# Strassen's seven half products for b in two of six pairs of ft tiles

## The chip, the cores and the metric

The kernel runs on one core of a Trainium2 chip. The metric is the device time of one execution in microseconds (us). Five engines work beside each other, each with its own in-order queue: TensorE (PE; PEld are its weight loads), VectorE (DVE), ScalarE (ACT), GpSimd (POOL), and SyncE (SP), which here issues nearly all DMAs.

## The reference

Chunked attention without a mask between chunks, then a bilinear feed-forward layer. Heads are merged to the 512 model columns, and all products are plain matrix products:

```python
# q, k, v: (8, 8, 576, 64), chunks of 64 rows
scores = scale * np.matmul(q_c, k_c.transpose(0, 1, 2, 4, 3))
scores = scores - np.max(scores, axis=-1, keepdims=True)
attn = np.exp(scores)
attn = attn / (np.sum(attn, axis=-1, keepdims=True) + 1e-09)
out = np.matmul(attn, v_c)
...
# x: (4608, 512) from out; w_a, w_b: (512, 1536); w_out: (1536, 512)
a = x @ w_a
b = x @ w_b
return (a * b @ w_out).astype(np.float32)
```

## The kernel before

The 4608 tokens are cut into nine blocks of 512 (K = 0 to 8), and each block into two units of 256 tokens (u = 0 to 17). Attention of a unit gives half of xT, the block's x with model columns on the partitions (four tiles of 128, index kt). Of the 1536 hidden columns there are twelve ft tiles of 128, held in six pairs of 256 (wa, wb, wo, ab2).

Each block takes fourteen steps, s = 0 to 13. In steps 0 to 11 `ffn(K, ft)` makes one ft tile: four matmuls of 512 columns for b into one PSUM bank, four for a into the next (`ffn_products`, L399), then `ffn_close`: ScalarE casts b's bank to the bf16 tile bsb (L410), and VectorE multiplies a's bank by it into ab (L411). After every odd step VectorE makes `sum_ab` of the pair that is complete (L466 to L468), three sums that the output needs. In steps 12 and 13 `outs_fast` makes the output by Strassen's seven products of half size, with sums of ab and wo, 42 matmuls of 256 columns a step (L479), two copies by ScalarE, five adds by VectorE and three by GpSimd (L497). So the output product already has the form that the change gives to part of b.

All these products take their PSUM banks from a ring of four, F, in the order in which `nextF()` is called:

```python
    F = [pp.tile([128, 512], FP32, name=f"F{i}") for i in range(4)]
```

A product may start only when the bank that was handed out four requests earlier has been read. Semaphores for this and for all data are set from the order in which the program names the instructions; nothing is reordered, so the order within each engine's queue is the order of the program.

Attention of the next block lies between the steps. From block 3 on, `slot` comes after steps 1 and 8 (in block 2 after 4 and 9). It takes two banks of F for the sums of the exponentials (L252), makes the values into a separate bank pair PA (L268), has ScalarE take two logarithms (L278) and one reciprocal by the exponential (L282), and makes the scores of the following unit (L235). What comes behind it is put into a list `late`, and `step()` at the head of each following step issues one piece: the first normalise by VectorE (L287), the second, then ScalarE's exponential (L246):

```python
                    inverse(uv)
                    late.extend([(normalise, (uv, 0)), (normalise, (uv, 1))])
            if us is not None:
                scores(us, pairs)
                late.append((expo, (us,)))
```

A step after a slot GpSimd casts the q, k and v of the unit after next from f32 to bf16 (`cast_unit`, L170, 128x1024 each); two steps later SP issues the transposing DMA of q and k (`turn_unit`) and the loads of a later unit (`load_unit`).

Blocks 0 and 1 run an older form of the loops, with the loading of the weights, and are not touched by the change. The staging buffer wsta of the weights, ten parts of 1024 f32 columns, is taken over after that by wsum and asum, the sums for the outputs, in its parts 2 to 9; parts 0 and 1 lie idle.

Of the kernel before, what the change touches and what calls it, by code (L numbers as in the profile page):

```python
# [11 lines left out]
def kernel(  # L12
# [10 lines left out]
    nc = tc.nc  # L23
    BF16 = mybir.dt.bfloat16
    FP32 = mybir.dt.float32
    AF = mybir.ActivationFunctionType
    MULT = mybir.AluOpType.mult
    ADD = mybir.AluOpType.add
    SUB = mybir.AluOpType.subtract
# [7 lines left out]
    NKT = DM // 128  # L37
    NFT = DFF // 128
    BLK = 512
    NBLK = NTOK // BLK  # L40
    NU = NTOK // 256
# [5 lines left out]
    def buf(name, shape, dt):  # L47
        return sb.tile(shape, dt, name=name)
# [4 lines left out]
    for K in range(NBLK):  # L53
        if K == REST:
            chunks += [(b, 512) for b in range(B)]
        else:
            b = K if K < REST else K - 1
# [19 lines left out]
    xT = [buf(f"xT_{i}", [128, NKT, BLK], BF16) for i in range(3)]  # L77
# [5 lines left out]
    ab = [ab2[i // 2][:, i % 2, :] for i in range(NFT)]  # L83
    wa = [buf(f"wa_{i}", [128, NKT, 256], BF16) for i in range(NP)]
    wb = [buf(f"wb_{i}", [128, NKT, 256], BF16) for i in range(NP)]
    wo = [buf(f"wo_{i}", [128, 2, DM], BF16) for i in range(NP)]
    NWS = 10
    wsta = buf("wst", [128, NWS * 1024], FP32)
# [8 lines left out]
    asum = wsta[:, 6 * 1024:10 * 1024].bitcast(BF16)[:, 0:NP * 5 * HF]  # L97
    asum = asum.rearrange("p (i n t) -> p i n t", i=NP, n=5)
    part = buf("part", [128, 2, 5, HF], FP32)

    state = {"f": 0, "b": 0, "o": 0, "w": 6}

    def ring(name, bufs):
        i = state[name]
        state[name] = i + 1
        return bufs[i % len(bufs)]

    def nextF():
        return ring("f", F)
# [63 lines left out]
    def cast_qk(u, x, eng):  # L173
        copy(eng, qkb[u % 2][:, x, :], f32[u % NF32][x])
# [11 lines left out]
    def cast_v(u, eng, pieces=1):  # L186
        n = 1024 // pieces
        for i in range(pieces):
            copy(eng, vb[u % 3][:, n * i:n * i + n], f32[u % NF32][2][:, n * i:n * i + n])
# [203 lines left out]
    def ffn_products(K, ft, us, kts, banks, of="ba"):  # L393
        n = 256 * len(us)
        x = xT[K % 3]
        for m in of:
            w, bank = (wb, banks[0]) if m == "b" else (wa, banks[1])
            for kt in kts:
                nc.tensor.matmul(  # L399
                    bank[:, 0:n],  # L400
                    w[ft // 2][:, kt, (ft % 2) * 128:(ft % 2) * 128 + 128],
                    x[:, kt, us[0] * 256:us[0] * 256 + n],
                    start=(kt == 0),
                    stop=(kt == NKT - 1),
                )
# [9 lines left out]
    def ffn(K, ft, us=(0, 1)):  # L415
        banks = nextF(), nextF()
        ffn_products(K, ft, us, range(NKT), banks)
        ffn_close(K, ft, us, banks)
# [40 lines left out]
            c0, c1, op = ((1, 3, SUB), (2, 0, SUB), (0, 3, ADD))[part - 1]  # L459
            eng.tensor_tensor(out=y[:, part + 1], in0=b[:, c0], in1=b[:, c1], op=op)  # L460

    def sum_ab(i):

        a = ab2[i].rearrange("p f (h t) -> p (f h) t", h=2)
        y = asum[:, i]
        nc.vector.tensor_tensor(out=y[:, 4], in0=a[:, 0], in1=a[:, 3], op=ADD)  # L466
        nc.vector.tensor_tensor(out=y[:, 0:2], in0=a[:, 0:2], in1=a[:, 2:4], op=ADD)  # L467
        nc.vector.tensor_tensor(out=y[:, 2:4], in0=a[:, 1:3], in1=a[:, 0:4:3], op=SUB)  # L468

    def outs_fast(K, t):  # L470
        c = t * 128
        m3, m4, w, y1, y2 = [part[:, t, n, :] for n in range(5)]
        oa, ob = ring("o", osb), ring("o", osb)
        V, A, G = nc.vector, nc.scalar, nc.gpsimd

        def product(a, b, o=None, pairs=range(NP)):
            o = nextF()[:, 0:HF] if o is None else o
            for i in pairs:
                nc.tensor.matmul(  # L479
                    o, a(i)[:, c:c + 128], b(i), start=(i == 0), stop=(i == NP - 1)  # L480
                )
            return o

        def of_ab(f, h):
            return lambda i: ab2[i][:, f, h * HF:(h + 1) * HF]

        def of_wo(f, h):
            return lambda i: wo[i][:, f, h * HF:(h + 1) * HF]

        def of_asum(n):  # L490
            return lambda i: asum[:, i, n]

        def of_wsum(n):
            return lambda i: wsum[:, i, n]

        def add(eng, out, in0, in1, op=ADD):
            eng.tensor_tensor(out=out, in0=in0, in1=in1, op=op)  # L497

        if K == NBLK - 1 and t == 1:

            A.copy(out=m3, in_=product(of_ab(0, 0), of_wsum(2)))
            A.copy(out=m4, in_=product(of_ab(1, 1), of_wsum(3)))
            add(G, w, m3, m4)
            add(V, oa[:, HF:DM], product(of_asum(0), of_wo(1, 1)), m3)
            add(G, y1, w, oa[:, HF:DM], SUB)
            add(V, ob[:, 0:HF], product(of_asum(1), of_wo(0, 0)), m4)
            add(G, y2, w, ob[:, 0:HF], SUB)
            p1 = product(of_asum(4), of_wsum(4))
            store(K, 2 + t, ob, 0, HF)
            add(V, y1, p1, y1)  # L510
            add(V, oa[:, 0:HF], product(of_asum(3), of_wsum(1)), y1)
            store(K, t, oa)
            add(V, y2, p1, y2)
            add(V, ob[:, HF:DM], product(of_asum(2), of_wsum(0)), y2)
            store(K, 2 + t, ob, HF)
            return
        A.copy(out=m3, in_=product(of_ab(0, 0), of_wsum(2)))

        p4 = product(of_ab(1, 1), of_wsum(3), None, range(NP - 1))
        p1 = product(of_asum(4), of_wsum(4), None, range(NP - 1))  # L520
        product(of_ab(1, 1), of_wsum(3), p4, (NP - 1,))
        product(of_asum(4), of_wsum(4), p1, (NP - 1,))
        A.copy(out=m4, in_=p4)  # L523
        add(G, w, m3, m4)
        add(V, w, p1, w)
        add(V, oa[:, HF:DM], product(of_asum(0), of_wo(1, 1)), m3)
        add(G, y1, w, oa[:, HF:DM], SUB)
        add(V, ob[:, 0:HF], product(of_asum(1), of_wo(0, 0)), m4)
        add(G, y2, w, ob[:, 0:HF], SUB)
        add(V, oa[:, 0:HF], product(of_asum(3), of_wsum(1)), y1)  # L530
        store(K, t, oa)
        add(V, ob[:, HF:DM], product(of_asum(2), of_wsum(0)), y2)
        store(K, 2 + t, ob)
# [16 lines left out]
    with tc.manual_schedule():  # L550
# [4 lines left out]
        V, A, G = nc.vector, nc.scalar, nc.gpsimd  # L555
# [123 lines left out]
        def load_unit(u, xs=(0, 1, 2)):  # L679
            for x in once("load", u, xs):  # L680
                load_natural(u, x, (q, k, v)[x], nc.sync)

        def cast_unit(u, xs=(0, 1, 2)):
            for x in once("cast", u, xs):
                if x < 2:
                    cast_qk(u, x, G)
                else:
                    cast_v(u, G)

        def turn_unit(u):  # L690
            for _ in once("turn", u, (0,)):
                transpose_dma(u, nc.sync)
# [11 lines left out]
        def slot(uv, us, pairs=False, short=False):  # L704


            drain()
            if uv is not None:
                SU = nextF(), nextF()
                sums(uv, SU)  # L710
                values(uv)
                log_sums(uv, SU)
                if short:
                    for cl in range(2):
                        late.extend([(inverse, (uv, cl)), (normalise, (uv, cl))])
                else:
# [6 lines that stand above are left out]
        def step():  # L723
            if late:
                fn, a = late.pop(0)
                fn(*a)
# [45 lines left out]
        for f0 in range(0, NFT, 2):  # L772

            for tgs in ((0, 1), (2, 3)):
# [3 lines left out]
                if (f0, tgs[0]) == (2, 0):  # L778
                    t = [transpose_pairs(2, x, (PS, PA)[x][:, 0, :]) for x in range(2)]
# [83 lines left out]
        slots = {}  # L863
        for K in range(2, NBLK):
            for s0, u in zip((4, 9) if K == 2 else (1, 8), (2 * K + 3, 2 * K + 4)):
                slots[K * (NFT + 2) + s0] = u
        for K in range(2, NBLK):
            for s in range(NFT + 2):
                step()
                if s < NFT:  # L870
                    ffn(K, s)
                    if s % 2:
                        sum_ab(s // 2)
                else:
                    outs_fast(K, s - NFT)
                if (K, s) == (2, 0):
                    slot(None, 6)
                i = K * (NFT + 2) + s
                if i in slots and slots[i] - 1 < NU:
                    slot(slots[i] - 1, slots[i] if slots[i] < NU else None)  # L880
                if i - 1 in slots:

                    cast_unit(slots[i - 1] + 1, (0, 1) if slots[i - 1] == 8 else (0, 1, 2))
                if i - 5 in slots:
                    cast_unit(slots[i - 5] + 1)
                if i - 3 in slots:
                    turn_unit(slots[i - 3] + 1)
                    load_unit(slots[i - 3] + 3)


# [28 lines left out]
```

## Time and profile before

| | |
|---|---|
| median of three runs | 314.49 us (312.73 to 314.68) |
| the profiled execution | 314.75 us, its span 313.0 us |
| TensorE busy | 303.3 us, 97% |
| VectorE busy | 187.1 us, 60% |
| ScalarE busy | 135.0 us, 43% |
| GpSimd busy | 124.4 us, 40% |
| granted TensorE clock | 1.000 |

In the lines of the profile, a row of a group names the line, engine and operation, what is written and read, the shapes, the count, the busy time, the mean of one in ns, and after the second bar the idle time of the engine before these instructions with its releaser. A row of the timeline gives the start in us from the span's start, the duration, the engine and line, and in brackets the time that the engine stood idle before. A row of the chain gives start, duration, engine and line. Matmul records overlap, since matmuls are pipelined; a pace is read from the distance of starts.

### The profile page before, as it was taken

The numbers are of one execution on the slowest core, as the hardware profiler recorded it, in microseconds if no ns is written. First come the engines' busy times: TensorE is split into PE (matmuls) and PEld (weight loads), VectorE is DVE, ScalarE is ACT, GpSimd is POOL, SyncE is SP. The second block draws the span as 40 slices with busy tenths as digits, with TensorE's granted clock in tenths as the row PEclk, the third lists the DMA queues.
The fourth block names the chain that finished last, engine by engine and source line by source line (L and its number), as shares of the span: only waits on it lengthen the run. The fifth ranks groups of instructions, "written<-read, shape, count | busy, mean of one in ns | idle before, by whom it ended". The sixth has DMA issues, their size and how long they took to land.

```text
span 313.0 us, 7353 instructions
## 1 busy us (share of the span) xinstructions
PE 303.3 (97%) x2924; PEld 177.9 (57%) x2924; DVE 187.1 (60%) x373; ACT 135.0 (43%) x232; POOL 124.4 (40%) x155
## 2 busy tenths in 40 slices
PE   7898989999999999999999999999999999999995
PEld 3433446885444486447644764467446744674474
DVE  3543324544449664966496749674967476646664
ACT  3833236746236533553265326541644164413320
POOL 2676857966666137402630264016500400040013
PEclk9999999999999999999999999999999999999999
DMA  7999999999999999989699239933500320021003
GB/s 260 282 310 385 376 281 259 224 219 266 233 225 265 225 222 259 238 191 199 208 246 237 55 137 212 240 88 136 134 2 2 82 55 0 3 90 46 0 1 136
DMA packets 144915, 55.01 MB, mean 176 GB/s; under 512 B 126320, under 2 KB 138864, under 8 KB 144880
## 3 DMA queue, kind: packets, MB, share of 16 engines
q1 hardware_dynamic: 143792, 53.49, 68.3%
q10 hardware_dynamic: 1088, 1.05, 1.0%
q8 instruction: 23, 0.38, 0.5%
q14 instruction: 12, 0.10, 0.1%
HBM read 37.75 MB, written 9.44 MB: 151 GB/s over the span
## 4 chain that ended last, share of the span: by engine, by line
PE 85%; DMA 9%; SPq 3%; DVE 1%; issue 1%; POOL 0%; ACTq 0%; DVEq 0%
PE F L399 53%; PE F L479 20%; PE F L421 6%; DMA f<-in_k_dram 5%; DMA wst<-in_moe_w_b_dram 4%; SPq L155 2%; PE F L252 2%; PE PS L235 2%; PE PA L268 1%; SPq L147 1%; SPq L160 0%; POOL wb L170 0%; ACTq L140 0%; PE F L195 0%; DVE osb L497 0%
## 5 line engine op out<-in xcount | busy, mean ns | idle before, releaser
L399 PE MATMUL F<-xT,wa 128*128 128x512 bf16 (+1 forms) x472 | 115.0, 361 | 1.3 <-POOL wa L170 1.0
L399 PE MATMUL F<-xT,wb 128*128 128x512 bf16 (+1 forms) x472 | 115.4, 361 | 0.9 <-DVE xT L385 0.9
L410 ACT CAST bsb<-F 128x512 bf16<-128x512 f32 (+1 forms) x118 | 64.4, 547 | 104.6 <-PE F L399 104.4
L411 DVE TENSOR_TENSOR ab<-F,bsb 128x512 bf16<-128x512 f32 (+1 forms) x118 | 75.7, 643 | 52.1 <-PE F L399 38.0
L399 PEld LDWEIGHTS <-wa 128*128 128x128 bf16 x472 | 45.9, 98 | 50.2 <-POOL wa L170 3.2
L399 PEld LDWEIGHTS <-wb 128*128 128x128 bf16 x472 | 44.6, 98 | 43.7 <-POOL wb L170 0.8
L497 POOL TENSOR_TENSOR part<-part 128x256 f32<-128x256 f32 x14 | 10.1, 724 | 129.7 <-ACT part L523 128.6
L170 POOL CAST qkb<-f 128x1024 bf16<-128x1024 f32 (+1 forms) x35 | 34.6, 1002 | 24.1 <-DMA f<-in_q_dram 13.8
L479 PEld LDWEIGHTS <-wst 128*128 128x128 bf16 x420 | 41.1, 98 | 4.8
L287 DVE TENSOR_TENSOR xT<-PA,inv 128x512 bf16<-128x512 f32 x32 | 21.8, 684 | 19.4 <-ACT inv L282 19.4
L479 PE MATMUL F<-wst 128*128 128x256 bf16 x252 | 33.3, 273 | 0.0
L497 DVE TENSOR_TENSOR osb<-F,part 128x256 f32<-128x256 f32 x56 | 22.4, 420 | 11.2 <-POOL part L497 9.7
L497 POOL TENSOR_TENSOR part<-part,osb 128x256 f32<-128x256 f32 x28 | 19.7, 725 | 11.4 <-DVE osb L497 11.3
L170 POOL CAST vb<-f 128x1024 bf16<-128x1024 f32 (+2 forms) x22 | 20.1, 917 | 10.0 <-DMA f<-in_v_dram 10.0
L479 PE MATMUL F<-wst,ab 128*128 128x256 bf16 x168 | 22.8, 273 | 0.0
L467 DVE TENSOR_TENSOR wst<-ab 128x512 bf16<-128x512 bf16 x42 | 22.3, 530 | 0.0
L421 PE MATMUL F<-wo,ab 128*128 128x512 bf16 x96 | 21.7, 379 | 0.0
L468 DVE TENSOR_TENSOR wst<-ab 128x512 bf16<-128x512 bf16 x42 | 21.4, 510 | 0.0
L246 ACT ACTIVATE E<-PS 128x1024 bf16<-128x1024 f32 (+1 forms) x20 | 18.8, 942 | 5.1 <-PE PS L235 3.5
L278 ACT ACTIVATE lns<-F 128x512 f32<-128x512 f32 x30 | 16.3, 595 | 10.3 <-PE F L252 10.3
L479 PE MATMUL F<-wo,wst 128*128 128x256 bf16 x168 | 20.6, 273 | 0.0
L497 DVE TENSOR_TENSOR part<-F,part 128x256 f32<-128x256 f32 x15 | 6.4, 424 | 21.1 <-POOL part L497 21.1
(62 smaller groups left out, 195.5 us busy)
## 6 DMA issues: line engine op xcount, KB each, us to landing
out_dram<-osb SPq DMA_DIRECT2D x31, 256.0 KB, 2.6
f<-in_q_dram SPq DMA_DIRECT2D x28, 256.0 KB, 4.1
f<-in_v_dram SPq DMA_DIRECT2D x28, 256.0 KB, 4.7
f<-in_k_dram SPq DMA_DIRECT2D x24, 256.0 KB, 4.2
wst<-in_moe_w_out_dram SPq DMA_DIRECT2D x6, 512.0 KB, 8.8
f<-in_v_dram SPq DMA_DIRECT2D x16, 128.0 KB, 3.8
wst<-in_moe_w_b_dram SPq DMA_DIRECT2D x8, 256.0 KB, 5.2
wst<-in_moe_w_a_dram SPq DMA_DIRECT2D x8, 256.0 KB, 5.2
```

Source lines behind the costliest of these rows:

```text
L170: eng.tensor_copy(out=out, in_=in_)
L246: nc.scalar.activation(out=e[:, :, s], in_=PS[:, :, s], func=AF.Exp, scale=scale)
L278: nc.scalar.activation(out=lns[:, cl, :], in_=SU[cl], func=AF.Ln)
L287: nc.vector.tensor_tensor(out=x.rearrange("p m (g c t) -> p c g m t", g=2, c=2)[:, cl], in0=PA[:, cl, :].rearrange(shape, g=2, m=4), in1=i ...
L399: nc.tensor.matmul(bank[:, 0:n], w[ft // 2][:, kt, (ft % 2) * 128:(ft % 2) * 128 + 128], x[:, kt, us[0] * 256:us[0] * 256 + n], start=(kt ...
L410: nc.scalar.copy(out=bT[:, 0:n], in_=banks[0][:, 0:n])
L411: nc.vector.tensor_tensor(out=ab[ft][:, us[0] * 256:us[0] * 256 + n], in0=banks[1][:, 0:n], in1=bT[:, 0:n], op=MULT)
L421: nc.tensor.matmul(o, ab[ft][:, tg * 128:(tg + 1) * 128], wo[ft // 2][:, ft % 2, :], start=(ft == 0), stop=(ft == NFT - 1),)
L467: nc.vector.tensor_tensor(out=y[:, 0:2], in0=a[:, 0:2], in1=a[:, 2:4], op=ADD)
L468: nc.vector.tensor_tensor(out=y[:, 2:4], in0=a[:, 1:3], in1=a[:, 0:4:3], op=SUB)
L479: nc.tensor.matmul(o, a(i)[:, c:c + 128], b(i), start=(i == 0), stop=(i == NP - 1))
L497: eng.tensor_tensor(out=out, in0=in0, in1=in1, op=op)
```

## The change

In blocks 3 to 8, b of the pairs 1 and 3 (ft tiles 2, 3 and 6, 7) is no longer made by four matmuls a tile. x is cut into halves of its tokens and of its model columns, the pair's weights into halves of model columns and of the two tiles, and b of both tiles is made by Strassen's seven products of half size, two matmuls of 256 columns each. `fast_b` does it in four stages, each with one bank of F:

- stage 0: two products; ScalarE copies both to f32, GpSimd adds them into m1
- stage 1: two products; VectorE adds them to the copies, into the middle half of bS
- stage 2: one product; VectorE adds it to m1, GpSimd makes two differences y12
- stage 3: two products; VectorE adds them to y12, into the outer quarters of bS

`with_b` then makes a of each of the two tiles as before, and VectorE multiplies it by bS, which is f32 and lies in SBUF; for these tiles there is no cast of b's bank. The stages lie between the other tiles in a list `work` of fourteen steps. The sums of weights are made once a pair by `sum_w` on GpSimd (pair 1 in block 2 at step 9, pair 3 at its end), the sums of x once a block by `sum_x`, also on GpSimd: 1 and 2 at step 11 of the block before, 0 and 3 at step 0. `sum_ab` can be issued in parts, and the list `ab_sums` says where. From block 3 on the casts of q and v go to ScalarE, q one step and v four steps after the cast of k, which stays on GpSimd. Block 2 keeps its order apart from the added sums.

```diff
+    spare = wsta[:, 0:2 * 1024].bitcast(BF16)
+    SP = (1, 3)
+    ws = {p: spare[:, i * 1280:i * 1280 + 1280].rearrange("p (n k c) -> p n k c", n=5, k=2)
+          for i, p in enumerate(SP)}
+    xs3 = spare[:, 2560:4096].rearrange("p (n k t) -> p n k t", n=3, k=2)
+    xs2 = buf("xs2", [128, 2, 2, 256], BF16)
+    xs = [xs3[:, 0], xs3[:, 1], xs3[:, 2], xs2[:, 0], xs2[:, 1]]
+    bS = buf("bS", [128, 2 * BLK], FP32)
...
-    def sum_ab(i):
+    def sum_ab(i, parts=(4, 0, 2)):
...
-        nc.vector.tensor_tensor(out=y[:, 4], in0=a[:, 0], in1=a[:, 3], op=ADD)
-        nc.vector.tensor_tensor(out=y[:, 0:2], in0=a[:, 0:2], in1=a[:, 2:4], op=ADD)
-        nc.vector.tensor_tensor(out=y[:, 2:4], in0=a[:, 1:3], in1=a[:, 0:4:3], op=SUB)
+        V = nc.vector
+        for part in parts:
+            if part == 4:
+                V.tensor_tensor(out=y[:, 4], in0=a[:, 0], in1=a[:, 3], op=ADD)
+            elif part == 0:
+                V.tensor_tensor(out=y[:, 0:2], in0=a[:, 0:2], in1=a[:, 2:4], op=ADD)
+            else:
+                V.tensor_tensor(out=y[:, 2:4], in0=a[:, 1:3], in1=a[:, 0:4:3], op=SUB)
+    def sum_w(p, eng):
+        w, y = wb[p], ws[p]
+        for out, in0, in1, op in (
+            (y[:, 0:2].rearrange("p n k c -> p k n c"),
+             w[:, 0:2].rearrange("p k (n c) -> p k n c", n=2),
+             w[:, 2:4].rearrange("p k (n c) -> p k n c", n=2), ADD),
+            (y[:, 2], w[:, 0:2, 0:128], w[:, 2:4, 128:256], ADD),
+            (y[:, 3], w[:, 0:2, 128:256], w[:, 0:2, 0:128], SUB),
+            (y[:, 4], w[:, 2:4, 0:128], w[:, 2:4, 128:256], SUB),
+        ):
+            eng.tensor_tensor(out=out, in0=in0, in1=in1, op=op)
+    def sum_x(K, n, eng):
+        x = xT[K % 3]
+        a, b = x[:, :, 0:256], x[:, :, 256:512]
+        out, in0, in1, op = (
+            (xs[0], a[:, 0:2], b[:, 2:4], ADD),
+            (xs[1], b[:, 0:2], b[:, 2:4], SUB),
+            (xs[2], a[:, 2:4], a[:, 0:2], SUB),
+            (xs2.rearrange("p n k t -> p (n k) t"), a, b, ADD),
+        )[n]
+        eng.tensor_tensor(out=out, in0=in0, in1=in1, op=op)
+    def fast_b(K, p, stage):
+        x, w, y = xT[K % 3], wb[p], ws[p]
+        V, A, G = nc.vector, nc.scalar, nc.gpsimd
+        m = part[:, SP.index(p)]
+        m34, m1, y12 = m[:, 0:2], m[:, 2], m[:, 3:5]
+        b4 = bS.rearrange("p (n c) -> p n c", n=4)
+        bank = nextF()
+        def product(h, a, b):
+            for k in range(2):
+                nc.tensor.matmul(
+                    bank[:, h * 256:h * 256 + 256], a[:, k], b[:, k], start=(k == 0), stop=(k == 1)
+                )
+        both = bank.rearrange("p (n c) -> p n c", n=2)
+        if stage == 0:
+            product(0, w[:, 0:2, 0:128], xs[1])
+            product(1, w[:, 2:4, 128:256], xs[2])
+            A.copy(out=m34, in_=both)
+            G.tensor_tensor(out=m1, in0=m34[:, 0], in1=m34[:, 1], op=ADD)
+        elif stage == 1:
+            product(0, y[:, 0], x[:, 2:4, 256:512])
+            product(1, y[:, 1], x[:, 0:2, 0:256])
+            V.tensor_tensor(out=b4[:, 1:3], in0=both, in1=m34, op=ADD)
+        elif stage == 2:
+            product(0, y[:, 2], xs[0])
+            V.tensor_tensor(out=m1, in0=bank[:, 0:256], in1=m1, op=ADD)
+            for n in range(2):
+                G.tensor_tensor(out=y12[:, n], in0=m1, in1=b4[:, 1 + n], op=SUB)
+        else:
+            product(0, y[:, 4], xs[4])
+            product(1, y[:, 3], xs[3])
+            V.tensor_tensor(out=b4[:, 0:4:3], in0=both, in1=y12, op=ADD)
+    def with_b(K, ft):
+        bank = nextF()
+        ffn_products(K, ft, (0, 1), range(NKT), (None, bank), "a")
+        c = (ft % 2) * BLK
+        nc.vector.tensor_tensor(out=ab[ft], in0=bank, in1=bS[:, c:c + BLK], op=MULT)
...
+        def queue_next_fast(i):
+            if i - 1 in slots:
+                cast_unit(slots[i - 1] + 1, (1,))
+            if i - 2 in slots:
+                cast_unit(slots[i - 2] + 1, (0,), A)
+            if i - 5 in slots:
+                cast_unit(slots[i - 5] + 1, (2,), A)
+            if i - 3 in slots:
+                turn_unit(slots[i - 3] + 1)
+                load_unit(slots[i - 3] + 3)
...
+            if s == 9:
+                sum_w(SP[0], G)
+            if s == NFT - 1:
+                sum_x(3, 1, G)
+                sum_x(3, 2, G)
...
+        sum_w(SP[1], G)
+        p, r = SP
+        work = [
+            [(ffn, 0), (fast_b, p, 0)],
+            [(ffn, 1)],
+            [(fast_b, p, 1), (fast_b, p, 2), (ffn, 4)],
+            [(fast_b, p, 3), (with_b, 2)],
+            [(with_b, 3), (fast_b, r, 0)],
+            [(ffn, 5)],
+            [(fast_b, r, 1), (fast_b, r, 2), (ffn, 8)],
+            [(fast_b, r, 3), (with_b, 6)],
+            [(with_b, 7)],
+            [(ffn, 9)],
+            [(ffn, 10)],
+            [(ffn, 11)],
+            [(outs_fast, 0)],
+            [(outs_fast, 1)],
+        ]
+        ab_sums = {4: [(0,)], 5: [(1,)], 6: [(2,)], 8: [(3, (4, 0))], 10: [(4, (4, 0))],
+                   11: [(5, (4, 0)), (3, (2,)), (4, (2,)), (5, (2,))]}
+        for K in range(3, NBLK):
+            for s, todo in enumerate(work):
+                step()
+                if s == 0:
+                    sum_x(K, 0, G)
+                for fn, *args in todo:
+                    fn(K, *args)
+                if s == 0:
+                    sum_x(K, 3, G)
+                if s == NFT - 1 and K + 1 < NBLK:
+                    sum_x(K + 1, 1, G)
+                    sum_x(K + 1, 2, G)
+                for a in ab_sums.get(s, ()):
+                    sum_ab(*a)
                 i = K * (NFT + 2) + s
+                slot_at(i)
+                queue_next_fast(i)
```

More of the change, by code (lines that the diff above doesn't have):

```diff
@@ L681, in load_unit, with cast_unit @@
                 load_natural(u, x, (q, k, v)[x], nc.sync)
-        def cast_unit(u, xs=(0, 1, 2)):
+        def cast_unit(u, xs=(0, 1, 2), eng=G):
             for x in once("cast", u, xs):
                 if x < 2:
-                    cast_qk(u, x, G)
+                    cast_qk(u, x, eng)
                 else:
-                    cast_v(u, G)
+                    cast_v(u, eng)
         def turn_unit(u):
@@ L866, with queue_next @@
                 slots[K * (NFT + 2) + s0] = u
-        for K in range(2, NBLK):
-            for s in range(NFT + 2):
-                step()
[L870 to L877, printed above, removed]
-                i = K * (NFT + 2) + s
[L879 to L888, printed above, removed]
+        def queue_next(i):
+            if i - 1 in slots:
+                cast_unit(slots[i - 1] + 1, (0, 1) if slots[i - 1] == 8 else (0, 1, 2))
+            if i - 5 in slots:
+                cast_unit(slots[i - 5] + 1)
+            if i - 3 in slots:
+                turn_unit(slots[i - 3] + 1)
+                load_unit(slots[i - 3] + 3)
@@ new lines, in queue_next_fast, with slot_at @@
+        def queue_next_fast(i):
+            if i - 1 in slots:
+                cast_unit(slots[i - 1] + 1, (1,))
+            if i - 2 in slots:
+                cast_unit(slots[i - 2] + 1, (0,), A)
+            if i - 5 in slots:
+                cast_unit(slots[i - 5] + 1, (2,), A)
+            if i - 3 in slots:
+                turn_unit(slots[i - 3] + 1)
+                load_unit(slots[i - 3] + 3)
+        def slot_at(i):
+            if i in slots and slots[i] - 1 < NU:
+                slot(slots[i] - 1, slots[i] if slots[i] < NU else None)
@@ new lines @@
+        for s in range(NFT + 2):
+            step()
+            if s < NFT:
+                ffn(2, s)
+                if s % 2:
+                    sum_ab(s // 2)
+            else:
+                outs_fast(2, s - NFT)
+            if s == 0:
+                slot(None, 6)
+            if s == 9:
[3 more added lines that the diff above has]
+                sum_x(3, 2, G)
+            i = 2 * (NFT + 2) + s
+            slot_at(i)
+            queue_next(i)
@@ new lines @@
+        ab_sums = {4: [(0,)], 5: [(1,)], 6: [(2,)], 8: [(3, (4, 0))], 10: [(4, (4, 0))],
+                   11: [(5, (4, 0)), (3, (2,)), (4, (2,)), (5, (2,))]}
+        for K in range(3, NBLK):
+            for s, todo in enumerate(work):
+                step()
+                if s == 0:
+                    sum_x(K, 0, G)
+                for fn, *args in todo:
+                    fn(K, *args)
+                if s == 0:
+                    sum_x(K, 3, G)
[4 more added lines that the diff above has]
+                    sum_ab(*a)
+                i = K * (NFT + 2) + s
+                slot_at(i)
+                queue_next_fast(i)
```

## The prediction

> **What bounds the kernel now.** I read the engine totals first, then the chain that ended last, then the waits and the timeline of blocks 3 to 5. From the page:
>
> ```profile
> PE 303.3 (97%) x2924; PEld 177.9 (57%) x2924; DVE 187.1 (60%) x373; ACT 135.0 (43%) x232; POOL 124.4 (40%) x155
> ...
> PE 85%; DMA 9%; SPq 3%; DVE 1%; issue 1%; POOL 0%; ACTq 0%; DVEq 0%
> PE F L399 53%; PE F L479 20%; PE F L421 6%; DMA f<-in_k_dram 5%; DMA wst<-in_moe_w_b_dram 4%; SPq L155 2%; PE F L252 2%; PE PS L235 2%; PE PA L268 1%; SPq L147 1%; SPq L160 0%; POOL wb L170 0%; ACTq L140 0%; PE F L195 0%; DVE osb L497 0%
> ```
>
> TensorE is the path. A full chain gives its pace:
>
> ```profile
> 143.17 9.17 PE F L479 x84
> 152.34 3.45 PE F L399 x16
> ...
> 175.10 9.17 PE F L479 x84
> ```
>
> Outputs start 31.93 us apart, the period of a block. A 512-column matmul takes 3.45/16 = 0.216 us, a 256-column one 9.17/84 = 0.109: half, so the weight loads stay hidden at 256 columns. An ffn tile is 1.73 us, a slot (sums, values, scores) 0.91.
>
> So only two things count: matmul columns saved, and waits that TensorE newly meets. It meets almost none now, because VectorE always empties a bank of the four-bank ring F in time. VectorE is not free at will, though:
>
> ```profile
> 168.83 0.41 PE L252 MATMUL F<-E,ones 64*64 64x512 bf16 x4
> ...
> 171.49 0.69 DVE L287 TENSOR_TENSOR xT<-PA,inv 128x512 bf16<-128x512 f32 x1 [1.79 <-ACT inv L282]
> 172.09 0.68 DVE L411 TENSOR_TENSOR ab<-F,bsb 128x512 bf16<-128x512 f32 x1
> ```
>
> The reader sees VectorE standing 1.79 us at the first normalise until ScalarE's reciprocal is there, 2.66 us after the sums began; the next instruction starts 0.60 later. And its bf16 sums stretch when GpSimd runs:
>
> ```profile
> 156.63 0.61 DVE L466 TENSOR_TENSOR wst<-ab 128x256 bf16<-128x256 bf16 x1
> 157.16 1.25 DVE L467 TENSOR_TENSOR wst<-ab 128x512 bf16<-128x512 bf16 x1
> 158.34 1.25 DVE L468 TENSOR_TENSOR wst<-ab 128x512 bf16<-128x512 bf16 x1
> ...
> 173.02 0.42 DVE L467 TENSOR_TENSOR wst<-ab 128x512 bf16<-128x512 bf16 x1
> ```
>
> The same sum takes 0.42 with GpSimd idle and 1.25 beside its casts (156.06 to 159.32).
>
> [...] each stretched sum ends shortly after one GpSimd cast; products that read PSUM keep 0.69. [...] the trace's 725 ns for 256 elements and 1269 for 512 (f32 in) give 2.13 ns each.
>
> **What the change removes and adds.** Blocks 3 to 8, two pairs each.
>
> TensorE: per pair eight 512-column matmuls (1.727 us) become fourteen of 256 (1.528): 0.20 saved, 0.40 a block, 2.4 in all. This is the whole possible gain.
>
> ScalarE, a block: four bank casts go (4 x 0.58), two copies come (2 x 0.59) and up to four casts of 128x1024. ScalarE has no such row; its exponential of that shape takes 1.03, taken for each (0.6 to 1.3 changes nothing below). It is 43% busy; nothing below waits for it. The moved casts hold back the transpose DMA on SP and the loads behind it, but the transpose is due half a block later.
>
> VectorE, a block: six new operations, four like L411 (0.69, next starts after 0.60) and two like the 256-column adds (0.42, after 0.33): about 3.1 us. None goes.
>
> GpSimd, a block: sum_x 3 x 1.27 + 2.36 (1024 elements by the slope) = 6.2; six adds of 0.725 = 4.35; four casts of 1.04 go while casts last. The bf16 input sums are not in the trace: by a cast's 1.04 per 1024 elements sum_x would be 2.6 in all, by a third more than the slope 8.2. I take 6.2, since the two-input rate is what the f32 rows show.
>
> **The schedule, by hand.** T = 0 at the sums of slot s1, blocks 3 to 7. A bank is reused four requests later.
>
> s2: stage 1 runs 0.91 to 1.35, stage 2 to 1.57, ffn(4) to 3.30. Stage 3 wants the bank of stage 1. VectorE empties that only behind the normalise: 2.66 + 0.60 = 3.26, end 3.95. TensorE waits **0.7**. Behind it VectorE does the m1 add (to 4.28), the product of ft 4 and the second normalise; GpSimd makes y12 from 4.33 to 5.74; VectorE's stage 3 add runs 5.8 to 6.5, ft 2 to 7.1, ft 3 to 7.7. TensorE: stage 3 to 4.44, ft 2 and 3 to 6.16, stage 0 of the second pair to 6.6, ffn(5) to 8.33.
>
> sum_ab(0) starts at 7.63 beside GpSimd's m1 add (7.43 to 8.15): free at 8.9, not 8.5. The product of ft 5 and sum_ab(1) follow, so stage 1's add of the second pair runs 10.4 to 11.1. TensorE has done stages 1, 2 and ffn(8) at 10.7 and wants that bank: **0.4**.
>
> Then m1, the product of ft 8 and sum_ab(2) from 11.9. GpSimd has y12 (11.46 to 12.9) and straight behind it the k cast (to 14.0; queued at s9 but with nothing to wait for), so the three sums each lose to one GpSimd instruction and end at 14.2 instead of 12.8. Stage 3's add ends at 14.9. The second bank of the sums in slot s8 is that bank; TensorE wants it at 13.5: **1.4** in blocks 3 to 6. In block 7, without casts, 14.1: **0.6**.
>
> s10 to s12: sum_x 1 and 2 (2.5 us) start behind the last normalise and block sum_ab(4), so ab of ft 11 and the last asum come some **0.3** after the outputs want them. The third sums that are deferred to s11 are not due before the sixth of the seven output products: hidden, at the price of one more 0.3 for each product by which they should be late.
>
> Block 8 has no slot and no casts: VectorE reaches stage 1's add at once, all banks are in time, the gain stays. Block 2 gets sum_w of pair 1 against sum_ab(3) and sum_x(3) against sum_ab(5): 0.5. sum_w of pair 3 (3.5 us) at the start of block 3 delays xs2 by 0.6 beyond the stage 3 wait. Together **1.1**.
>
> Sum: 5 x 0.7 + 5 x 0.4 + (4 x 1.4 + 0.6) + 5 x 0.3 + 1.1 - 2.4 = 11.9. The profiled execution took 314.75 (span 313.0 and 1.75 around it), so 326.65; the median of the runs lies 0.26 below it: 326.4.
>
> **Where the costs are uncertain.** The 0.7 is firm if the queue order is as written. [...] with GpSimd harmless to VectorE they shrink to about 0.2 a block (y12 alone). With sum_x at 8.2 or y12 pushed by VectorE's own turns, 0.5 to 1 more a block. The new VectorE operations with f32 outputs have no row of 512; below 0.60 none can come by the PSUM rate of L411, above 0.75 I see no reason for: +-0.3 a block.
>
> **Rivals.** (1) Only the normalise costs: [...]. Five blocks 0.7 + 0.2 - 0.4, block 8 -0.4, 1.0 for blocks 2 and 3: 314.5 + 3.1 = 317.6, half of its span inside 1%. For it: L467's mean of 530 ns over 42 says that most sums ran undisturbed. Against: y12 and the k cast fall exactly into sum_ab(2).
>
> (2) The other side: TensorE stays the path. Its mechanism is the four-bank ring: if each stage's bank is emptied within the next three requests, all new work lies beside matmuls, and 2.4 comes off: 312.1. It decides at stage 3 of the first pair: the stage 1 add must end by T + 3.3, that is, the reciprocal must come 0.7 earlier. For it: VectorE is 60% and GpSimd 40% busy, and ScalarE loses work. Against: ScalarE's two logarithms and the reciprocal before that normalise are not touched, so its 2.66 us stay.
>
> (3) GpSimd becomes the bound: sum_x at 8.2 a block, y12 queued behind it, stage 3 late everywhere; 1.5 a block more, 335.
>
> **How the numbers follow.** Forecast 0.55, rival 1 0.20, rival 2 0.15, rival 3 0.10. About 1% is what a measurement of this kernel can tell from no change. Faster by over 1% would need more than the whole saving: 0.02. Within 1% (311.3 to 317.6): the rest of rival 2 and half of rival 1, 0.23. Slower 0.75. The forecast's own range is 321 to 332; to leave no more than 2 in 10 out it takes in rival 1 (from 315) and the lower half of rival 3: 315 to 334.
>
> **What would show it.** Right: TensorE idle once per block 3 to 7 before stage 3 until VectorE's bS, and once before the sums of the second slot; VectorE's asum sums at a mean well over the 0.51 to 0.53 of before; GpSimd busy near 175 us (124 + 6 x 10.6 + two sum_w of 3.5 - 17 casts of 1.04), ScalarE near 146; block 8 shorter by 0.4. Wrong: no idle of TensorE at those places, a block of 31.5 us, or an idle that waits on GpSimd's xs or ScalarE's bank copies.

## The result, and the profile after

The changed kernel takes 328.89 us (median of six runs, 328.04 to 329.53) against 314.58 for the kernel before (six runs): a ratio of 1.0466, 95% interval 1.0434 to 1.0497. It is slower by 14.3 us; 326.4 was forecast, in a range of 315 to 334. The span of the profiled execution grew from 313.0 to 327.7.

First the page of the changed kernel: busy times, then the chain that ended last, by engine and by line.

```profile
PE 307.1 (94%) x2996; PEld 185.2 (56%) x2996; DVE 217.0 (66%) x409; ACT 144.1 (44%) x237; POOL 174.5 (53%) x206
...
PE 47%; DVE 15%; ACT 4%; issue 3%; DVEq 0%
PE F L410 23%; PE F L564 19%; PE F L524 3%; DVE wst L484 3%; DVE wst L482 2%; DVE wst L480 2%; ACT lns L289 2%; DVE ab L553 2%; ACT inv L293 2%; DVE ab L422 2%; DVE bS L537 2%; PE F L263 1%; DVE bS L546 1%; PE PA L279 1%; DVE part L540 1%
```

Before, the chain was TensorE's for 85%, and VectorE had 1% of it. Now VectorE has 15%: its sums of ab (L480 to L484), its stage adds (L537, L540, L546) and its products (L422, and L553 for the tiles with bS) stand between two matmuls. Lines have moved by the inserted code: L410 are the ffn products, L524 the stages, L564 the outputs, L263 the sums of a slot.

The chain in order of time for one block (start, duration, engine, line) shows where it leaves TensorE:

```profile
148.55 7.60 PE F L564 x67
...
160.05 0.39 PE F L263 x4
160.44 1.08 ACT lns L289 x2
161.53 0.02 issue
161.55 1.06 ACT inv L293
...
163.25 0.69 DVE bS L537
163.94 0.05 issue
163.98 0.61 PE F L524 x4
...
166.57 1.29 DVE ab L553 x2
...
174.51 0.61 DVE bS L546
175.12 0.04 issue
175.16 0.22 PE F L263
...
183.42 7.60 PE F L564 x67
```

The period is 183.42 - 148.55 = 34.87 us, against 31.93 before: 2.94 more in each of the blocks 3 to 6. Inside it the chain goes twice through VectorE to a bank of F; the second time it stays there from 166.57 to 175.12, with VectorE's instructions back to back. The waits of TensorE in the timeline (in brackets the idle time; matmul records overlap, so the loss of pace is larger than the bracket):

```profile
162.64 0.69 DVE L298 TENSOR_TENSOR xT<-PA,inv 128x512 bf16<-128x512 f32 x1 [1.79 <-ACT inv L293]
163.25 0.68 DVE L537 TENSOR_TENSOR bS<-F,part 128x512 f32<-128x512 f32 x1
...
163.98 0.61 PE L524 MATMUL F<-xs,wst 128*128 128x256 bf16 x4 [0.54 <-DVE bS L537]
...
171.24 0.60 PE L524 MATMUL F<-xs,wst 128*128 128x256 bf16 x4 [0.37 <-DVE bS L537]
...
175.16 0.41 PE L263 MATMUL F<-E,ones 64*64 64x512 bf16 x3 [1.27 <-DVE bS L546]
```

The first: ffn(4) began at 161.56 and at its pace was through at 163.29; stage 3 starts at 163.98, 0.70 late. L537, which frees its bank, starts just 0.61 after the normalise, and that stood 1.79 us until the reciprocal, as long as the one at 171.49 in the kernel before. The second: ffn(8) began at 168.98, so stage 3 of the second pair is due at 170.71 and starts at 171.24, 0.53 late. The third: the slot's sums begin at 173.49, the second bank comes at 175.16, and the next ffn starts at 176.06 in place of 173.49 + 0.91: 1.65 late.

Why the third is so long is seen on VectorE and GpSimd just before (L542 are the two differences y12, L181 is the k cast):

```profile
171.59 1.46 POOL L542 TENSOR_TENSOR part<-part,bS 128x256 f32<-128x256 f32 x2 [3.30 <-DVE part L540]
...
172.04 0.43 DVE L480 TENSOR_TENSOR wst<-ab 128x256 bf16<-128x256 bf16 x1
172.39 0.94 DVE L482 TENSOR_TENSOR wst<-ab 128x512 bf16<-128x512 bf16 x1
173.00 1.23 POOL L181 CAST qkb<-f 128x1024 bf16<-128x1024 f32 x1
173.25 1.25 DVE L484 TENSOR_TENSOR wst<-ab 128x512 bf16<-128x512 bf16 x1
174.43 0.68 DVE L546 TENSOR_TENSOR bS<-F,part 128x512 f32<-128x512 f32 x1
```

Each of the three sums ends shortly after one GpSimd instruction: two differences y12 and the k cast. They take 0.43, 0.94 and 1.25 where the same sums take 0.29, 0.42 and 0.42 with GpSimd idle, and L546, the add that frees the bank, stands behind them.

The fourth loss lies at the start of the outputs, which take 9.60 us instead of 9.17:

```profile
179.84 2.31 POOL L512 TENSOR_TENSOR wst<-xT 128x512 bf16<-128x512 bf16 x2 [5.61 <-DVE xT L298]
...
180.41 0.74 DVE L480 TENSOR_TENSOR wst<-ab 128x256 bf16<-128x256 bf16 x1
...
181.07 1.37 DVE L482 TENSOR_TENSOR wst<-ab 128x512 bf16<-128x512 bf16 x1
...
183.09 0.10 PEld L564 LDWEIGHTS <-ab 128*128 128x128 bf16 x1 [0.21 <-DVE ab L422]
183.42 2.74 PEld L564 LDWEIGHTS <-wst 128*128 128x128 bf16 x25 [0.23 <-DVE wst L480]
```

The sums of x for the next block on GpSimd (L512) stretch sum_ab(4), so the product of ft 11 comes late, and behind it the first sum of the last pair. TensorE waits for both, 0.21 and 0.23 us.

### The profile page after: what moved, and what is told of

Same layout as the page of the kernel before. It is cut to its first block, busy times and chain, and to the rows that moved or that the text cites. A ratio compares the mean times of both kernels' runs of the same rounds, so it can differ in the third digit from the quotient of the medians.

```text
span 327.7 us, 7608 instructions
## 1 busy us (share of the span) xinstructions
PE 307.1 (94%) x2996; PEld 185.2 (56%) x2996; DVE 217.0 (66%) x409; ACT 144.1 (44%) x237; POOL 174.5 (53%) x206
## 4 chain that ended last, share of the span: by engine, by line
PE 47%; DVE 15%; ACT 4%; issue 3%; DVEq 0%
PE F L410 23%; PE F L564 19%; PE F L524 3%; DVE wst L484 3%; DVE wst L482 2%; DVE wst L480 2%; ACT lns L289 2%; DVE ab L553 2%; ACT inv L293 2%; DVE ab L422 2%; DVE bS L537 2%; PE F L263 1%; DVE bS L546 1%; PE PA L279 1%; DVE part L540 1%
## 5 line engine op out<-in xcount | busy, mean ns | idle before, releaser
L410 PE MATMUL F<-xT,wa 128*128 128x512 bf16 (+1 forms) x472 | 113.1, 361 | 0.9 <-DVE ab L422 0.7
L410 PE MATMUL F<-xT,wb 128*128 128x512 bf16 (+1 forms) x376 | 90.7, 357 | 1.0 <-DVE xT L396 0.9
L422 DVE TENSOR_TENSOR ab<-F,bsb 128x512 bf16<-128x512 f32 (+1 forms) x94 | 59.0, 630 | 41.1 <-PE F L410 25.2
L421 ACT CAST bsb<-F 128x512 bf16<-128x512 f32 (+1 forms) x94 | 50.5, 539 | 75.5 <-PE F L410 75.1
L410 PEld LDWEIGHTS <-wa 128*128 128x128 bf16 x472 | 46.1, 98 | 46.9 <-issue 1.9
L410 PEld LDWEIGHTS <-wb 128*128 128x128 bf16 x376 | 35.7, 98 | 28.5 <-POOL wb L181 0.6
L564 PEld LDWEIGHTS <-wst 128*128 128x128 bf16 x420 | 40.5, 98 | 7.0 <-DVE wst L480 1.1
L181 POOL CAST qkb<-f 128x1024 bf16<-128x1024 f32 (+1 forms) x27 | 27.5, 1019 | 19.5 <-DMA f<-in_q_dram 11.8
L512 POOL TENSOR_TENSOR wst<-xT 128x512 bf16<-128x512 bf16 x18 | 20.8, 1171 | 30.3 <-DVE xT L298 30.3
L564 PE MATMUL F<-wst 128*128 128x256 bf16 x252 | 34.3, 273 | 0.2
L542 POOL TENSOR_TENSOR part<-part,bS 128x256 f32<-128x256 f32 x24 | 17.2, 737 | 29.5 <-DVE part L540 22.9
L482 DVE TENSOR_TENSOR wst<-ab 128x512 bf16<-128x512 bf16 x42 | 27.3, 651 | 0.0
L582 POOL TENSOR_TENSOR part<-part 128x256 f32<-128x256 f32 x14 | 11.8, 844 | 27.0 <-ACT part L608 25.9
L484 DVE TENSOR_TENSOR wst<-ab 128x512 bf16<-128x512 bf16 x42 | 25.4, 627 | 0.0
L564 PE MATMUL F<-wst,ab 128*128 128x256 bf16 x168 | 22.8, 273 | 0.0
L564 PE MATMUL F<-wo,wst 128*128 128x256 bf16 x168 | 20.8, 273 | 0.3 <-DVE wst L482 0.3
```

What stands on the lines that cost most here:

```text
L181: eng.tensor_copy(out=out, in_=in_)
L410: nc.tensor.matmul(bank[:, 0:n], w[ft // 2][:, kt, (ft % 2) * 128:(ft % 2) * 128 + 128], x[:, kt, us[0] * 256:us[0] * 256 + n], start=(kt ...
L421: nc.scalar.copy(out=bT[:, 0:n], in_=banks[0][:, 0:n])
L422: nc.vector.tensor_tensor(out=ab[ft][:, us[0] * 256:us[0] * 256 + n], in0=banks[1][:, 0:n], in1=bT[:, 0:n], op=MULT)
L482: V.tensor_tensor(out=y[:, 0:2], in0=a[:, 0:2], in1=a[:, 2:4], op=ADD)
L484: V.tensor_tensor(out=y[:, 2:4], in0=a[:, 1:3], in1=a[:, 0:4:3], op=SUB)
```

## The experiments

The theory under test: TensorE loses at four places, each because VectorE's queue empties a bank (or delivers an ab) late; the first is made by the order in that queue alone, the other three by the order and by sums of VectorE that are stretched while GpSimd runs (0.42 us became 0.94 and 1.25 in the rows above), together. The rivals: GpSimd's total load, ScalarE's new casts, or the latency of four stages as such. The ratio is against the kernel before, run beside each experiment. The line numbers stay near those of the changed kernel.

The changed kernel itself was not run again beside the experiments, and the kernel before differs by up to 0.7 us between sessions, so the distance of a median from 328.89 is that uncertain. A second measure is the trace: from the first output matmul of block 2 to that of block 8 the changed kernel takes 203.61 us (111.49 to 315.10), the kernel before 189.23 (111.08 to 300.31). No experiment changes anything ahead of this stretch, and yet their profiled executions reach it anywhere between 109.0 and 112.0 us. Below, "in the stretch" gives the difference of this measure.

**The normalise behind the stage adds (e1).**

```diff
-            [(fast_b, p, 1), (fast_b, p, 2), (ffn, 4)],
+            [(fast_b, p, 1), (fast_b, p, 2), (late_step,), (ffn, 4)],
...
-                step()
+                if s != 2:
+                    step()
```

`late_step(K)` calls `step()`. 

> Undoes one order: in step 2 of blocks 3 to 8 the first normalise is put behind the VectorE adds of stages 1 and 2. Queue theory (the stage 1 bank is emptied late only because the add stands behind a normalise that waits 1.79 us for the reciprocal): the wait of 0.70 us before stage 3 goes, and since everything behind starts 1.6 earlier, most of the 0.53 before the second pair's stage 3 goes too; the wait in the second slot stays, since y12 and the k cast on GpSimd still meet sum_ab(2). Five blocks by 1.2: 328.9 - 6 = 323. Rival (GpSimd's own work, or the latency of the four stages from engine to engine, sets the pace whatever the order on VectorE): under 1 us.

Measured 324.62 us, ratio 1.0332 (1.0292 to 1.0372): 4.3 less than the changed kernel, 4.0 less in the stretch; 323 was expected. In its timeline:

```profile
159.62 0.69 DVE L537 TENSOR_TENSOR bS<-F,part 128x512 f32<-128x512 f32 x1 [0.69 <-PE F L524]
...
160.72 0.69 DVE L298 TENSOR_TENSOR xT<-PA,inv 128x512 bf16<-128x512 f32 x1
...
161.36 0.60 PE L524 MATMUL F<-xs,wst 128*128 128x256 bf16 x4
...
168.43 0.60 PE L524 MATMUL F<-xs,wst 128*128 128x256 bf16 x4 [0.20 <-DVE bS L537]
```

The wait before stage 3 has gone (no bracket at 161.36), at no price: the normalise starts as soon as its reciprocal is there. The period falls from 34.87 to 33.98, that is 0.89 a block, and 0.70 of it is this wait. Of the second wait less went than I had expected, 0.17 of 0.53: sum_ab(0) and sum_ab(1) still stand before that add, and one of them now takes 0.95 beside GpSimd's m1 add. The third wait stays at 1.27, as expected.

**sum_ab(2) behind the second stage 3 (e2).**

```diff
-        ab_sums = {4: [(0,)], 5: [(1,)], 6: [(2,)], 8: [(3, (4, 0))], 10: ...
+        ab_sums = {4: [(0,)], 5: [(1,)], 8: [(2,), (3, (4, 0))], 10: ...
```

> Undoes another order: sum_ab(2) moves from step 6 to step 8, behind the stage 3 add of the second pair and the product of ft 7. Queue theory: the stage 3 add then waits for y12 alone (about 13.0 us after the first slot's sums, end 13.65 in place of 15.0), so the wait of 1.65 in the second slot falls to 0.2 or 0.3 in blocks 3 to 6 and from about 1.0 to 0.2 in block 7: 328.9 - 6.5 = 322.4. Rival (y12 itself is late because GpSimd has too much to do): no change, since GpSimd's list is not touched; below 1 us.

Measured 322.13, ratio 1.0255 (1.0221 to 1.0290): 6.8 less, 6.1 less in the stretch, the period 33.48.

```profile
169.27 1.41 POOL L542 TENSOR_TENSOR part<-part,bS 128x256 f32<-128x256 f32 x2 [3.30 <-DVE part L540]
170.62 1.04 POOL L181 CAST qkb<-f 128x1024 bf16<-128x1024 f32 x1
170.71 0.69 DVE L546 TENSOR_TENSOR bS<-F,part 128x512 f32<-128x512 f32 x1 [0.93 <-POOL part L542]
171.16 0.70 PE L263 MATMUL F<-E,ones 64*64 64x512 bf16 x4
```

The add starts as soon as y12 is there, and the slot's sums run nearly through: the next ffn is 0.29 late in place of 1.65. The k cast beside an operation that reads PSUM costs that nothing (0.69). The first two waits are as in the changed kernel. GpSimd's list is the same, so its load is not what holds this place.

**No k cast in the second slot (e3).**

```diff
-            if i - 1 in slots:
+            if i - 1 in slots and i % (NFT + 2) < 8:
                 cast_unit(slots[i - 1] + 1, (1,))
```

> Leaves out the k cast of the second slot in blocks 3 to 6 (four casts of 128x1024 on GpSimd; the scores of those units are made from old data). [...] the last of the three sums of sum_ab(2) no longer loses to that cast (1.25 becomes 0.42), stage 3's add comes 0.8 earlier, the wait in the second slot falls from 1.65 to about 0.85 in four blocks: 328.9 - 3.3 = 325.6. Rival ([...] the sums are just ahead in the queue): no change, since nothing waits for this cast itself within a block.

Measured 324.98, ratio 1.0347 (1.0319 to 1.0376): 3.9 less, 3.4 less in the stretch. Its timeline has the last of the three sums and the third wait at

```profile
171.03 0.41 DVE L484 TENSOR_TENSOR wst<-ab 128x512 bf16<-128x512 bf16 x1
172.09 0.41 PE L263 MATMUL F<-E,ones 64*64 64x512 bf16 x3 [0.43 <-DVE bS L546]
```

The sum takes 0.41 where it took 1.25, and the wait is 0.43 where it was 1.27: 0.84 less in four blocks is 3.4. Nothing in the block waits for this cast, and the sums ahead of L484 take what they took (0.43, 0.94), so the gain comes from the sum that the cast had kept waiting. This prices the meeting on this kernel: one GpSimd cast in the wrong place costs 0.84 us of TensorE. The runs show that the sum is held up beside the cast; what in the chip holds it they don't show.

**All casts on GpSimd again (e4).**

```diff
-                queue_next_fast(i)
+                queue_next(i)
```

> Undoes the second part of the change alone: from block 3 on q, k and v are all cast by GpSimd as before. [...] in step 2 three casts (3.1 us) follow y12 and push the m1 add of the second pair and meet sum_ab(0) and sum_ab(1); in step 9 they meet sum_ab(3) besides sum_ab(2). About 0.5 to 1 us more a block in four blocks: 331 to 333. Rival (the casts don't matter, only VectorE's queue order): within 0.5 us of 328.9. Should the moved casts hold up ScalarE instead: 1 to 2 us faster.

Measured 332.52, ratio 1.0583 (1.0546 to 1.0620): 3.6 more, 4.0 more in the stretch. The period is 35.79, and a new wait appears in the middle of ffn(8), behind sums of ab that now meet the casts:

```profile
170.71 1.02 PE L410 MATMUL F<-xT,wa 128*128 128x512 bf16 x4 [0.68 <-DVE ab L422]
```

So the moved casts help, and ScalarE's new casts are not what holds the changed kernel up: the loss is in the other part.

**Both orders together (e5).** The edits of e1 and e2. 

> The two reorderings of VectorE's queue together: the normalise behind the adds of stages 1 and 2, and sum_ab(2) at step 8. If the two waits are separate links (queue theory), the gains add up: in blocks 3 to 6 the period falls by 0.9 and 1.4, to about 32.6 us against 31.9 before, because a wait of 0.3 before the second stage 3, one of 0.2 in the slot and 0.4 at the outputs are left: about 317. If one wait only hides the other, no better than the better of the two alone (322).

Measured 318.11, ratio 1.0146 (1.0106 to 1.0185); the period is 32.61, as expected; 317 was expected in all. The two gains add: in the stretch 4.0 and 6.1 alone, 10.0 together. They are separate links, neither hides the other.

**One pair only (e7).** `work` without the four stages of pair 3, whose two ft tiles are made by `ffn`; no sum_w of pair 3. 

> One part of the change alone: only pair 1 goes through the four stages, pair 3 is made by eight 512-column matmuls and two casts as before. Theory: the 0.70 before stage 3 and the 0.43 at the outputs stay, the waits of the second pair (0.53 and 1.65) go, and half of the saving too: 0.93 a block in five blocks, 0.5 in block 2, -0.2 in block 8: 314.2 + 5.0 = 319. If the loss were shared by the two pairs alike: 321 to 322.

Measured 319.06, ratio 1.0172 (1.0130 to 1.0215), period 32.88: 0.95 above the kernel before, against 0.70 + 0.43 - 0.20 = 0.93. The list of waits (us in total, times, longest):

```profile
PE F L524 <- DVE bS L537: 2.7, 5, 0.5
PEld L564 <- DVE ab L422: 1.3, 5, 0.5
PEld L564 <- DVE wst L480: 1.2, 5, 0.2
```

Five stage 3 waits are left, and the ones at the outputs; those of 0.53 and 1.65 have gone. The second pair thus brought 9.8 of the 14.3 us (9.1 in the stretch).

**The sums of x on VectorE (e8).**

```diff
-                if s == 0:
-                    sum_x(K, 0, G)
...
-                if s == 0:
-                    sum_x(K, 3, G)
-                if s == NFT - 1 and K + 1 < NBLK:
-                    sum_x(K + 1, 1, G)
-                    sum_x(K + 1, 2, G)
+                if s >= NFT and K + 1 < NBLK:
+                    for n in ((1, 2), (0, 3))[s - NFT]:
+                        sum_x(K + 1, n, V)
```

In block 2 the first two sums move likewise, and the other two, for block 3, come into its last step.

> Takes away one load of GpSimd: the sums of x (5.6 us a block) are made by VectorE in the output steps; all else as in the changed kernel. [...] only the 0.43 at the outputs goes (sum_x met sum_ab(4) there), in five blocks and in block 2: 328.9 - 2.6 = 326.3. Rival (GpSimd's total load is what holds things up): the waits behind y12 shrink as well, 5 us or more.

Measured 326.34, ratio 1.0402 (1.0365 to 1.0439): 2.6 less, 2.4 less in the stretch, with 5.6 us a block taken off GpSimd. The outputs take 9.27 instead of 9.60; the other three waits stay as they were:

```profile
161.96 0.60 PE L524 MATMUL F<-xs,wst 128*128 128x256 bf16 x4 [0.53 <-DVE bS L537]
169.20 0.60 PE L524 MATMUL F<-xs,wst 128*128 128x256 bf16 x4 [0.37 <-DVE bS L537]
173.13 0.41 PE L263 MATMUL F<-E,ones 64*64 64x512 bf16 x3 [1.27 <-DVE bS L546]
```

GpSimd's load as such is not the bound; what counts is which VectorE sum it meets. Here e2 and e8 agree: the one left GpSimd's list as it was and gained 6.8, the other took 5.6 us a block off it and gained only at the place where the sums met.

**All waits addressed (e6).** The edits of e1 and e8, and

```diff
-        ab_sums = {4: [(0,)], 5: [(1,)], 6: [(2,)], 8: [(3, (4, 0))], 10: ...
+        ab_sums = {4: [(0,)], 8: [(1,), (2,)], 9: [(3, (4, 0))], 10: ...
```

> The same products with every wait found so far addressed: the normalise behind the stage 1 and 2 adds, sum_ab(1) and sum_ab(2) at step 8 and sum_ab(3) at step 9, and all sums of x made by VectorE in the output steps, where it stands idle for 1.8 us. If the list of waits is complete, TensorE meets no new wait and the saving of 0.40 us a block shows: six blocks by 0.4 off, block 2 unchanged: 312.0, ratio 0.993 to 0.995. If GpSimd or ScalarE had been a bound of their own (rival), some 2 to 5 us of the loss stay: 317 to 319.

Measured 311.91 (ten runs), ratio 0.9930 (0.9907 to 0.9953): faster than the kernel before by 0.7%, with an interval clear of 1. The chain is TensorE's again:

```profile
140.79 9.27 PE F L564 x84
150.06 1.73 PE F L410 x8
151.78 0.44 PE F L524 x4
...
172.41 9.27 PE F L564 x84
```

The period is 31.62, 0.31 under the kernel before: the saving of 0.40 less 0.10 that the outputs still lose. Six blocks of that are 1.9 us; 1.9 is what the stretch shows against the kernel before, and 2.1 the medians. The four stages and ScalarE's casts are all still there, so neither these casts nor the latency between the stages has to cost more than that 0.10.

**The same with all casts on GpSimd (e9).** e6 with the edit of e4. 

> The reordered kernel (e6) with all three casts back on GpSimd from block 3 on. Asks what the second part of the change is worth once the queue is in order. [...] the casts (3.1 us each time) follow y12 and now meet sum_ab(0), push the second pair's m1 add by about 2 us, and meet the three sums at step 8: VectorE's later sums start up to 2 us late, before the normalise of the second slot, with about 1 us of slack there; 0.3 to 0.8 us a block in four blocks: 313 to 315 against 312. Rival (with nothing on the path behind them, the casts are free on either engine): within 0.5 us of 312.

Measured 313.78, ratio 0.9981 (0.9962 to 0.9999), against the 0.9930 of e6 taken in another session; the intervals don't overlap, narrowly. Its period is 31.90: the casts meet the first of the sums at step 8, VectorE arrives at the outputs late, and the product of ft 11 and its sum are waited for as in the changed kernel, 0.2 us each:

```profile
176.14 0.55 PEld L564 LDWEIGHTS <-ab 128*128 128x128 bf16 x6 [0.20 <-DVE ab L422]
...
177.60 2.74 PEld L564 LDWEIGHTS <-wst 128*128 128x128 bf16 x25 [0.23 <-DVE wst L480]
```

Four blocks by 0.28 are 1.1 of the 1.9 us between the medians of e6 and e9, and the stretch is longer by just these 1.1. The traces show no other loss: what else the two profiled executions differ by lies ahead of the stretch, which e6 reaches at 109.0 and e9 at 112.0, with the same instructions until there. So the casts on GpSimd cost about 1.1 of the 1.9 us that e6 gains; the second part of the change keeps them.

## Why the prediction was right, point by point

It was right in direction, in size and in the mechanism of the main losses; its sum was 2.4 us short. By its own steps:

- The saving: 0.40 a block. In the trace, the stages of the second pair take 0.44 to 0.66 us for four or six matmuls, 0.109 each, and e6, where nearly no wait is left, shows 0.31 of it.
- The wait before stage 3: 0.7 forecast, 0.70 measured; e1 took it away and showed its cause.
- The wait before the second stage 3: 0.4 forecast, 0.53 measured. The add stands behind sum_ab(0) and sum_ab(1), as worked out, and sum_ab(0) took 1.25 us where 1.27 was forecast. The 0.13 was there before: the products of ft 2 and 3 ended 7.88 us after the slot's sums began, not 7.7.
- The wait in the second slot: 1.4 forecast, 1.65 measured. TensorE wanted the bank 13.5 us after the first slot's sums, as forecast; VectorE's add ended at 15.1 and not 14.9. About half of that came with the second wait (y12 began at 11.61 instead of 11.46). The rest is the k cast: it took 1.23 us beside the sums, where it takes 1.04 in e2 without them and 1.1 was forecast. I had only VectorE's sum slowed where the two meet, although in the kernel before the v cast beside the stretched L468 already takes 1.23 (at 158.09). In block 7, without casts, 0.6 was forecast and 1.0 measured: the slot's sums begin at 278.09 and the next ffn at 279.72, 1.63 later, where it was 0.62 before. The bank is 0.83 late, as in e3; the other 0.2 is unexplained.
- The outputs: 0.3 forecast, 0.43 measured (0.56 in block 7); e8 took away all but 0.1.
- Block 8: 0.4 faster forecast, 0.24 measured (20.48 us to its outputs against 20.72). Not all banks were in time: the second pair's stage 3 started 0.10 late, at 307.70.
- Blocks 2 and 3: 1.1 forecast, 0.9 found, but that they nearly agree is luck. 0.47 was found at the outputs of block 2, by the meeting of sum_x with sum_ab(5), as forecast. The 0.6 that the sums of weights were to cost in block 3 did not come: their four instructions took 3.0 and 3.4 us and met sums with slack behind them, and the wait before stage 3 in block 3 is the 0.54 of the other blocks. In its place 0.4 lies in a part of block 2 before any changed instruction, where loads arrived at other times; that is the spread between executions, and no effect of the change.

Put together: 5 x (0.70 + 0.53) + 4 x 0.43 + 0.56 + 4 x 1.65 + 1.0 + 0.47 + 0.4 - 5 x 0.40 - 0.24 = 14.7, the 14.7 by which the span grew. The term that rests on the queue's order alone was exact. The third wait was mis-sized most, 0.25 in four blocks and 0.4 in block 7. The busy times came as forecast too: GpSimd 174.5 us (175), ScalarE 144.1 (146), the new VectorE adds of 512 columns with f32 outputs 680 and 685 ns (L537, L546; 0.69 us was taken), and the sums of ab of 512 columns at means of 651 and 627 ns, up from 530 and 510:

```profile
L482 DVE TENSOR_TENSOR wst<-ab 128x512 bf16<-128x512 bf16 x42 | 27.3, 651 | 0.0
L484 DVE TENSOR_TENSOR wst<-ab 128x512 bf16<-128x512 bf16 x42 | 25.4, 627 | 0.0
```

The rivals: the mild one (317.6) failed because sums and GpSimd did meet in the same places in blocks 3 to 6. The one in which all is hidden (312.1) is what e6 reached (311.9): it was not ruled out by the amount of work added but by its place. The point that the prediction named for it, the reciprocal in front of the stage 1 add, is only part of that: e1 alone brought 4.3 of the 14.3 us, e1 and e2 together 10.8, and e6 also moved the sums of x to VectorE and more sums of ab back. GpSimd as the bound was refuted by e2 and e8.

## What to carry to other kernels

VectorE was 60% busy, and new work on it was still not free. Ask what stands in front of it in that engine's queue when the bank it frees is wanted, and put an instruction that waits for a slow chain behind those that are ready (e1: 4.3 us less). This kernel's ring of four banks gives each evacuation three requests of time; cutting a product into more, smaller stages shortens that time (0.22 or 0.44 us of matmuls a request instead of 0.86) while adding work to those who must meet it. Where a bank waits behind them, VectorE's sums with two SBUF inputs and GpSimd's adds and casts should be placed at different times: here 0.42 us became 0.94 and 1.25, and 0.41 again without the cast (e3). The VectorE operations of 512 columns that read PSUM kept their 0.69 us beside GpSimd (0.693 at most in the changed kernel).

## What the runs showed of the hardware that was not expected

GpSimd adds two bf16 tensors faster than the f32 rows suggested: 1171 ns for 128x512 and 2128 for 128x1024, that is 1.87 ns for each further element instead of 2.13. A block's sums of x took 5.6 us on GpSimd where the prediction had 6.2. On VectorE the same sum of 512 takes 0.42 us. And where the two meet, GpSimd is slowed too: its cast of 1.04 us (e2) took 1.23, and the outputs' first GpSimd add 1.02 instead of 0.72, beside VectorE's sums.
